# Taking the float64 weight conversion of an attention and MoE kernel in sixths of its columns

## The chip, the cores and the metric

The kernel runs on one core of one Trainium2 chip. The time is the device time of one execution in microseconds; the number to predict is the median of several runs of the changed kernel.

## The reference, cut to what matters

```python
# attention: q, k, v are (4, 12, 448, 64) float32
scores = scale * q @ k^T, causal mask, softmax over the last axis
attn_out = attn @ v
# MoE with a rational activation: x is (1792, 768)
x = attn_out.transpose(0, 2, 1, 3).reshape(1792, 768)
h = x @ w_in                        # w_in (768, 2048), float64
P = a0 + a1*h + a2*h^2 + a3*h^3
Q = 1 + |b0|*|h| + |b1|*h^2
g = P / (Q + 1e-6)
out = (g @ w_out).astype(float32)   # w_out (2048, 768), float64
```

The two weight matrices come as float64. The kernel reads them as pairs of 32-bit words and builds float32 values from the words by hand.

## The kernel before, in words

The kernel has an attention stage and an MoE stage. The attention stage loops over 24 head pairs (`NP`), one iteration per pair, and each iteration issues a list of small tasks in the order of the string `ORDER` (`attend`, L947; the first three iterations use `FIRST`, `SECOND` and `THIRD`). A task `name.arg@lag` works on the pair of the iteration less the lag. So one iteration holds, for different pairs: transposes of q and k (`qk`, psA), the scores (`s`, psS, L328), their maxima on VectorE (`m`, L339), the exponentials on ScalarE (`e`, L349), the reciprocal of the sums on VectorE (`r`, L359, with a small GpSimd op ahead of it, L356), the scaling of the exponentials on GpSimd (`n`, seven instructions, L366), their transposes on TensorE (`c`, psC, L385) with copies out of PSUM on VectorE (`v`, L397) and ScalarE (`a`, L395), the product with v (`d`, psD, L409) and its transfer to the MoE input (`dh` on ScalarE, `dl` on VectorE, L437 and L439).

Beside this, the attention stage converts the first weight blocks ("items") from float64 to float32. One item is a block of 128 x 768 values, loaded as `raw`, 128 x 768 x 2 words (`conv_load`, L143, three buffers). It takes two steps, `n` = 2 and `n` = 3 in the list `steps` (L444). Step 2 needs a GpSimd op on `raw` (L169, it leaves the sign in `u`) and then one VectorE instruction (L179) that joins the low word's top bits to `u`. Step 3 needs a GpSimd op (L173, it scales the high word in place by a power of two) and then one VectorE instruction (L185) that joins the shifted high word to `u`. Both VectorE instructions have two inputs in SBUF.

Which steps belong to which iteration is told by `quota` (L441): one whole step in iterations 3 to 15, 17, 19 and 21, and none in the others, 16 steps in all (eight items; items 8 and 9 are converted in the list `TAIL`). In an iteration the GpSimd op of its step is issued early (`cv.0`), which on GpSimd's queue is right behind the seven scalings of the iteration before; the VectorE instruction is issued last (`cv.2`), so on VectorE it stands between the last maximum and the next iteration's copies of psC. `cv.1` takes the first half of the iteration's steps, which is none where there is one. When an item is finished, the buffer is free and the load of the item three later is issued in the next iteration (`cv.3`). All DMAs go through SyncE's queue, in program order. The order on each engine is the order of the tasks, since the stage is scheduled by hand (`manual_schedule`, L893).

The MoE stage follows with matmuls that keep TensorE busy to the end, with the remaining weight blocks converted beside them.

Of the kernel before, what the change touches and what calls it, by code (L numbers as in the profile page):

```python
# [8 lines left out]
F32 = mybir.dt.float32  # L9
F32R = mybir.dt.float32r  # L10
U32 = mybir.dt.uint32
AF = mybir.ActivationFunctionType
ALU = mybir.AluOpType
# [3 lines left out]

ORDER = """
c.1@2 e.6@1 c.0@2 e.0@1 lv@-1 v.1@2 cv.0 dh@3 qk@-1 ld@-4 cv.3 a.1@2 sm@1 v.0@2 s.2 a.0@2 r@1 dl@3 qy@-1 n.2@1 s.3 qx@-1
n.3@1 m.3 m.4 s.0 n.5@1 s.1 e.3 m.5 d@2 n.0@1 e.4 n.4@1 m.0 e.5 m.1 n.6@1 m.2 e.1 m.6 n.1@1 e.2 cv.1 cv.2  # L20
"""


# [36 lines left out]
def kernel(  # L60
# [11 lines left out]
    nc = tc.nc  # L72
    B, H, S, D = q.shape
    DM, DFF = moe_w_in.shape
    P = 128
# [12 lines left out]
    NC = 10  # L88
    NR = 3
    NL = 3  # L90
# [6 lines left out]
    cv = ctx.enter_context(tc.tile_pool(name="cv", bufs=1))  # L97
# [43 lines left out]
    c_raw, c_u, c_32, stored = {}, {}, {}, set()  # L141

    def conv_load(m):  # L143
        if m >= len(items):
            return
        f, n = items[m]
        raw = c_raw[m] = cv.tile([P, DM, 2], U32, tag="raw", bufs=NR, name="raw64")
        if n == 0:
            nc.sync.dma_start(
                out=raw.rearrange("p (c f) t -> p c (f t)", c=KD),  # L150
                in_=moe_w_in[:, f * P:(f + 1) * P].bitcast(U32).rearrange("(c p) f -> p c f", p=P),
            )
        else:
            nc.sync.dma_start(
                out=raw.rearrange("p m t -> p (m t)"), in_=moe_w_out[f * P:(f + 1) * P, :].bitcast(U32)
            )

    def conv_step(m, s):
        raw = c_raw[m]
        yu = raw[:, :, 1]  # L160
        y = yu.bitcast(F32)
        if s == 1:
            if m in kept:
                u = xq.tile([P, K3 * NT], U32, tag=f"c{kept.index(m)}", name="u")[:, :DM]
            else:
                pool, tag, bufs = (lv, f"u{m}", 1) if NL <= m < NC - 3 else (cv, "u", 3)
                u = pool.tile([P, DM], U32, tag=tag, bufs=bufs, name="u")
            c_u[m] = u
            nc.gpsimd.tensor_scalar(  # L169
                out=u.bitcast(F32), in0=y, scalar1=0.0, scalar2=1.0, op0=ALU.mult, op1=ALU.mult  # L170
            )
        elif s == 5:
            nc.gpsimd.tensor_scalar(  # L173
                out=y, in0=y, scalar1=2.0 ** -112, scalar2=1.0, op0=ALU.mult, op1=ALU.mult
            )
        elif s == 4:
            nc.scalar.activation(out=y, in_=y, func=AF.Copy, scale=2.0 ** -112)
        elif s == 2:
            nc.vector.scalar_tensor_tensor(  # L179
                out=c_u[m], in0=raw[:, :, 0], scalar=29, in1=c_u[m],  # L180
                op0=ALU.logical_shift_right, op1=ALU.bitwise_or,
            )
        else:
            o = cv.tile([P, DM], F32, tag="ld", bufs=NL, name="w").bitcast(U32) if m < NL else c_u[m]
            nc.vector.scalar_tensor_tensor(  # L185
                out=o, in0=yu, scalar=3, in1=c_u[m], op0=ALU.logical_shift_left, op1=ALU.bitwise_or
            )
            c_32[m] = o.bitcast(F32)

    def conv_store(m):  # L190
        nc.sync.dma_start(out=w32[items[m]], in_=c_32[m])
# [58 lines left out]
    raw, QK, AT, pv, SUM, REC, psa, pss, psr, psc, nmx = {}, {}, {}, {}, {}, {}, {}, {}, {}, {}, {}  # L250
# [25 lines left out]
    def half(j):  # L276
        return slice(j * D, (j + 1) * D)
# [155 lines left out]
    def d_lo(p):  # L433
        ps = pv.pop(p)
        for r, hi, o in x_parts(p):
            if hi is not None:
                nc.vector.tensor_tensor(out=o, in0=ps[:, r], in1=hi.bitcast(F32), op=ALU.subtract)  # L437
            elif p % 2 == 0:
                nc.vector.tensor_copy(out=o, in_=ps[:, r])  # L439

    def quota(p):  # L441
        return int(3 <= p < 16 or p in (17, 19, 21))

    steps = [(m, n) for m in range(NC) for n in (2, 3)]  # L444
    done = []

    def conv(p, part):
        if part == 0:
            lo = sum(quota(x) for x in range(p))
            for m, n in steps[lo:lo + quota(p)]:  # L450
                conv_step(m, 1 if n == 2 else 5)
        elif part == 3:
            while done:
                conv_load(done.pop(0) + NR)
        else:
            lo = sum(quota(x) for x in range(p))
            mid, hi = lo + quota(p) // 2, lo + quota(p)
            for m, n in steps[lo:mid] if part == 1 else steps[mid:hi]:
                conv_step(m, n)
                if n == 3:  # L460
                    done.append(m)

    tasks = {
# [2 lines left out]
        "s": stage_b_pe, "m": stage_b_max, "e": stage_b_exp, "sm": stage_b_sum, "r": stage_b_rec, "n": stage_b_norm,  # L466
        "c": c_pe, "a": lambda p, h: c_ev(p, h, 0), "v": lambda p, h: c_ev(p, h, 1),
        "d": stage_d, "dh": d_hi, "dl": d_lo, "cv": conv,
    }

# [15 lines left out]
    tmp, g_t, acc, osb, part = {}, {}, {}, {}, {}  # L486
# [370 lines left out]
    def coeffs_done():  # L857
# [5 lines left out]
        "co": coeffs_done, "xr": close_r, "xl": close_l, "p1": p1, "p2": p2, "aa": act_a, "da": dve_a, "dz": dve_a3,  # L863
        "ab": act_b, "db": dve_b, "dy": dve_b3, "gh": g_hi, "gl": g_lo, "wh": w_hi, "wl": w_lo,
        "lw": load_w, "xa": lambda m: conv_step(m, 1), "xc": conv_step, "xs": conv_store, "xd": conv_load,
    })

# [25 lines left out]
    with tc.manual_schedule():  # L893
# [12 lines left out]
        ld = es_r.enter_context(pool(name="ld", bufs=2, side="right"))  # L906
# [7 lines left out]
        for x in range(2):  # L914
            m = mask[half(x), S - QB:]
            nc.gpsimd.affine_select(
                out=m, in_=m, compare_op=ALU.is_ge, fill=-1e9 / SCALE, base=0, pattern=[[-1, QB]], channel_multiplier=1,
# [51 lines left out]
        for t in range(2, NPL - 1):  # L969
            now = step.get(t, [])  # L970
# [57 lines left out]
        for j in range(HF):  # L1028
            n = j + 5
# [46 lines left out]
```

## Time and profile before

| | |
|---|---|
| median of 3 runs | 602.48 us (602.44 to 602.89) |
| the profiled execution | 602.94 us |
| its span | 601.1 us |
| TensorE busy | 594.0 us (99%) |
| VectorE busy | 535.9 us (89%) |
| ScalarE busy | 448.6 us (75%) |
| GpSimd busy | 169.2 us (28%) |
| TensorE's granted clock | 1.00 in both stages |

The span is the part of the execution that the profile covers. In the profile PE is TensorE, DVE is VectorE, ACT is ScalarE, POOL is GpSimd and SPq is the queue of SyncE, from which the DMAs are issued. A tile is named as the program names it, without its buffer number; L179 is line 179 of the kernel. Times of instructions are counted from the start of the span.

### The profile page before, as it was taken

Reading aid. Unit: us, or ns where it says so; the run is one execution under the profiler, and the core shown is the slowest. Engines: PE = TensorE matmul, PEld = TensorE weight load, DVE = VectorE, ACT = ScalarE, POOL = GpSimd, SP = SyncE. Lnnn points to the kernel's source line nnn. Section 1 sums busy time; section 2 is a strip of 40 time slices with the busy share of each in tenths; the row PEclk is TensorE's granted clock in tenths of the full one; section 3 lists DMA queues with packets and bytes.
Section 4 is the critical chain, followed back from the end, with each engine's and each line's share of the span. In section 5 each row is a group of like instructions: output and inputs, shape, how many; then the busy total and the mean of one; then the engine's idle time right before and its main releaser. Section 6 shows DMA issues by size and latency. Waiting matters only on the chain.

```text
span 601.1 us, 12762 instructions
## 1 busy us (share of the span) xinstructions
PE 594.0 (99%) x4660; PEld 494.2 (82%) x4660; DVE 535.9 (89%) x1015; ACT 448.6 (75%) x923; POOL 169.2 (28%) x266
## 2 busy tenths in 40 slices
PE   8999999999999999999999999999999999999997
PEld 6666666667888888888888888889999999998886
DVE  3999999988799999999999879998999999988950
ACT  4999999998877776668777776676477777677731
POOL 2899997766733401112333100000000000000000
PEclk9999999999999999999999999999999999999999
DMA  7979898776389988888985663443353344149872
GB/s 163 234 180 228 182 204 210 181 194 224 149 284 347 336 304 288 298 308 301 358 297 183 225 217 139 158 139 125 135 206 132 109 154 145 66 184 339 294 254 85
DMA packets 104863, 128.64 MB, mean 214 GB/s; under 512 B 70496, under 2 KB 82912, under 8 KB 104800
## 3 DMA queue, kind: packets, MB, share of 16 engines
q1 hardware_dynamic: 104800, 127.82, 67.2%
q8 instruction: 37, 0.61, 0.4%
q14 instruction: 26, 0.21, 0.1%
HBM read 98.31 MB, written 29.49 MB: 213 GB/s over the span
## 4 chain that ended last, share of the span: by engine, by line
PE 95%; DVE 2%; ACT 1%; POOL 1%; issue 0%; ACTq 0%
PE psO L614 25%; PE psH L242 22%; PE psQ L728 14%; PE psM L610 13%; PE psD L409 7%; PE psS L328 7%; PE psC L385 4%; PE psA L296 2%; PE psI L943 1%; ACT e L349 1%; POOL e L366 0%; DVE wq L707 0%; DVE xparts L637 0%; DVE p L528 0%; DVE at L397 0%
## 5 line engine op out<-in xcount | busy, mean ns | idle before, releaser
L614 PE MATMUL psO<-whl,gh 128*128 128x512 f32 x448 | 159.1, 391 | 0.0
L242 PE MATMUL psH<-xs,whl 128*128 128x512 f32 x576 | 136.7, 391 | 0.2 <-ACT e L349 0.2
L610 PE MATMUL psM<-whl,gh 128*128 128x256 f32 x448 | 126.2, 282 | 0.0
L242 PEld LDWEIGHTS psH<-xs,whl 128*128 128x128 f32 x576 | 105.9, 188 | 21.9 <-ACT e L349 0.3
L614 PEld LDWEIGHTS psO<-whl,gh 128*128 128x128 f32 x448 | 84.0, 188 | 17.8 <-ACT gh L540 0.4
L610 PEld LDWEIGHTS psM<-whl,gh 128*128 128x128 f32 x448 | 84.5, 189 | 1.7 <-DVE osb L598 0.3
L349 ACT ACTIVATE e<-psS,nm 128x448 f32<-128x448 f32 (+6 forms) x168 | 79.3, 568 | 4.3 <-DVE nm L339 3.2
L614 PE MATMUL psO<-whl,gl 128*128 128x512 f32 x224 | 81.1, 390 | 0.0
L728 PE MATMUL psQ<-xpart,wq 128*128 128x384 f32 x432 | 78.5, 336 | 0.1
L366 POOL TENSOR_SCALAR e<-e,r 128x192 f32<-128x192 f32 (+6 forms) x161 | 74.4, 487 | 13.9 <-DVE r L359 9.4
L728 PEld LDWEIGHTS psQ<-xpart,wq 128*128 128x128 f32 x432 | 74.8, 188 | 1.4 <-DVE hpair L754 0.4
L339 DVE CUSTOM_DVE_ANT_0 psS<-psS,mask 128x64 f32<-128x64 f32 (+6 forms) x168 | 65.4, 456 | 1.8 <-PE psS L328 1.3
L610 PE MATMUL psM<-whl,gl 128*128 128x256 f32 x224 | 63.2, 282 | 0.0
L169 POOL TENSOR_SCALAR u<-raw 128x768 f32<-128x768 f32 x32 | 36.9, 1153 | 57.6 <-DMA raw<-in_moe_w_out_dram 25.0
L517 ACT ACTIVATE w<-w 128x512 f32<-128x512 f32 x32 | 20.3, 633 | 39.8 <-DVE w L502 39.8
L614 PEld LDWEIGHTS psO<-whl,gl 128*128 128x128 f32 x224 | 42.0, 188 | 8.9
L328 PE MATMUL psS<-qkt 64*64 64x64 f32 (+6 forms) x672 | 47.5, 391 | 1.4 <-ACT e L349 1.2
L349 ACT ACTIVATION_READ_ACCUMULATOR e<-psS,nm 128x1 f32 x168 | 48.5, 299 | 0.0
L409 PE MATMUL psD<-at,vraw 128*64 128x448 f32 (+3 forms) x384 | 46.8, 386 | 0.0
L409 PEld LDWEIGHTS psD<-at,vraw 128*64 128x64 f32 x384 | 25.5, 136 | 24.9 <-issue 14.8
L610 PEld LDWEIGHTS psM<-whl,gl 128*128 128x128 f32 x224 | 42.3, 189 | 0.0
L328 PEld LDWEIGHTS psS<-qkt 64*64 64x64 f32 x672 | 21.3, 132 | 20.4 <-ACT at L395 10.7
(111 smaller groups left out, 1117.1 us busy)
## 6 DMA issues: line engine op xcount, KB each, us to landing
whl<-whl SPq DMA_DIRECT2D x64, 768.0 KB, 5.5
w<-w SPq DMA_DIRECT2D x51, 384.0 KB, 5.1
raw<-in_moe_w_in_dram SPq DMA_DIRECT2D x16, 768.0 KB, 5.4
raw<-in_moe_w_out_dram SPq DMA_DIRECT2D x16, 768.0 KB, 6.1
w<-u SPq DMA_DIRECT2D x26, 384.0 KB, 3.4
qraw<-in_q_dram SPq DMA_DIRECT2D x48, 112.0 KB, 3.5
kraw<-in_k_dram SPq DMA_DIRECT2D x48, 112.0 KB, 3.7
out_dram<-osb SPq DMA_DIRECT2D x13, 384.0 KB, 3.1
```

Source lines behind the costliest of these rows:

```text
L169: nc.gpsimd.tensor_scalar(out=u.bitcast(F32), in0=y, scalar1=0.0, scalar2=1.0, op0=ALU.mult, op1=ALU.mult)
L242: nc.tensor.matmul(ps, w[:, c * P:(c + 1) * P], xs[ck, part, c // K3][:, c % K3], start=(c == 0 and n == 0), stop=(c == KD - 1 and n == 2),)
L328: nc.tensor.matmul(pss[p, b][half((1 + b + j) % 2)], QK[p][half(j), 0, b * QB:(b + 1) * QB], QK[p][half(j), 1, :b_w[b]], start=True, stop= ...
L339: nc.vector.tensor_tensor_reduce(out=s, in0=s, in1=mask[:, S - w:], scale=-SCALE, scalar=3e38, op0=ALU.add, op1=ALU.min, accum_out=nmx[p][ ...
L349: nc.scalar.activation(out=E[p % 2][i][:, :w], in_=pss[p, i], func=AF.Exp, bias=nmx[p][:, i:i + 1], scale=-1.0, accum_out=SUM[p % 2][:, i: ...
L366: nc.gpsimd.tensor_scalar(out=e, in0=e, scalar1=REC[p][:, i:i + 1], scalar2=0.0, op0=ALU.mult, op1=ALU.add)
L385: nc.tensor.transpose(ps[x][:, slot // 2 * QB:(slot // 2 + 1) * QB], E[p % 2][n][r, lo:lo + P], ident[r, r])
L409: nc.tensor.matmul(ps[half(j), lo * QB:S], v[:, j, c], a[h][:, slot * QB:(slot + 7 - lo) * QB], start=(c == 0), stop=(c == 3), skip_group_ ...
L517: nc.scalar.activation(out=w, in_=w, func=AF.Abs)
L610: nc.tensor.matmul(acc["m", k], g, w[:, 512:], start=first and (k % 2 == 0 or each), stop=last, skip_group_check=True)
L614: nc.tensor.matmul(acc[k], g, w[:, :512], start=first, stop=last)
L728: nc.tensor.matmul(q_bank[j, bank], w[:, wp_, c * P:(c + 1) * P], xp_[:, c], start=(first and n == 0), stop=(n == 3 * K3 - 1), skip_group_ ...
```

## The change

The two VectorE instructions of a step can now be issued for a part of the columns, from `lo` to `hi`. The list `steps` holds each step six times, once for each sixth of its 768 columns, and `quota` counts sixths: five in iterations 3 to 12, six in 13, 14, 15, 17, 19 and 21, four in 16, three in 18 and 20 (96 sixths, the same 16 steps). In an iteration the sixths of one step are joined to one VectorE instruction; where an iteration's sixths belong to two steps, there are two instructions. The GpSimd op still covers all columns and is issued in the iteration in which the step begins. In iteration 18 the scaling of step 3 is done by VectorE (step number 6) ahead of its piece, and GpSimd has no such op. `cv.1`, which did nothing, is gone.

```diff
--- before.py
+++ after.py
@@ -17,7 +17,7 @@
 
 ORDER = """
 c.1@2 e.6@1 c.0@2 e.0@1 lv@-1 v.1@2 cv.0 dh@3 qk@-1 ld@-4 cv.3 a.1@2 sm@1 v.0@2 s.2 a.0@2 r@1 dl@3 qy@-1 n.2@1 s.3 qx@-1
-n.3@1 m.3 m.4 s.0 n.5@1 s.1 e.3 m.5 d@2 n.0@1 e.4 n.4@1 m.0 e.5 m.1 n.6@1 m.2 e.1 m.6 n.1@1 e.2 cv.1 cv.2
+n.3@1 m.3 m.4 s.0 n.5@1 s.1 e.3 m.5 d@2 n.0@1 e.4 n.4@1 m.0 e.5 m.1 n.6@1 m.2 e.1 m.6 n.1@1 e.2 cv.2
 """
 
 
@@ -155,9 +155,9 @@
                 out=raw.rearrange("p m t -> p (m t)"), in_=moe_w_out[f * P:(f + 1) * P, :].bitcast(U32)
             )
 
-    def conv_step(m, s):
+    def conv_step(m, s, lo=0, hi=DM):
         raw = c_raw[m]
-        yu = raw[:, :, 1]
+        yu = raw[:, lo:hi, 1]
         y = yu.bitcast(F32)
         if s == 1:
             if m in kept:
@@ -169,23 +169,25 @@
             nc.gpsimd.tensor_scalar(
                 out=u.bitcast(F32), in0=y, scalar1=0.0, scalar2=1.0, op0=ALU.mult, op1=ALU.mult
             )
-        elif s == 5:
-            nc.gpsimd.tensor_scalar(
+        elif s in (5, 6):
+            (nc.gpsimd if s == 5 else nc.vector).tensor_scalar(
                 out=y, in0=y, scalar1=2.0 ** -112, scalar2=1.0, op0=ALU.mult, op1=ALU.mult
             )
         elif s == 4:
             nc.scalar.activation(out=y, in_=y, func=AF.Copy, scale=2.0 ** -112)
         elif s == 2:
             nc.vector.scalar_tensor_tensor(
-                out=c_u[m], in0=raw[:, :, 0], scalar=29, in1=c_u[m],
+                out=c_u[m][:, lo:hi], in0=raw[:, lo:hi, 0], scalar=29, in1=c_u[m][:, lo:hi],
                 op0=ALU.logical_shift_right, op1=ALU.bitwise_or,
             )
         else:
-            o = cv.tile([P, DM], F32, tag="ld", bufs=NL, name="w").bitcast(U32) if m < NL else c_u[m]
+            if lo == 0:
+                o = cv.tile([P, DM], F32, tag="ld", bufs=NL, name="w") if m < NL else c_u[m].bitcast(F32)
+                c_32[m] = o
             nc.vector.scalar_tensor_tensor(
-                out=o, in0=yu, scalar=3, in1=c_u[m], op0=ALU.logical_shift_left, op1=ALU.bitwise_or
-            )
-            c_32[m] = o.bitcast(F32)
+                out=c_32[m][:, lo:hi].bitcast(U32), in0=yu, scalar=3, in1=c_u[m][:, lo:hi],
+                op0=ALU.logical_shift_left, op1=ALU.bitwise_or,
+            )
 
     def conv_store(m):
         nc.sync.dma_start(out=w32[items[m]], in_=c_32[m])
@@ -438,26 +440,37 @@
             elif p % 2 == 0:
                 nc.vector.tensor_copy(out=o, in_=ps[:, r])
 
+    NQ = 6
+
     def quota(p):
-        return int(3 <= p < 16 or p in (17, 19, 21))
-
-    steps = [(m, n) for m in range(NC) for n in (2, 3)]
+        if 3 <= p < 13:
+            return 5
+        if p in (13, 14, 15, 17, 19, 21):
+            return 6
+        return {16: 4, 18: 3, 20: 3}.get(p, 0)
+
+    steps = [(m, n, i) for m in range(NC) for n in (2, 3) for i in range(NQ)]
     done = []
 
     def conv(p, part):
+        lo = sum(quota(x) for x in range(p))
+        now = steps[lo:lo + quota(p)]
         if part == 0:
-            lo = sum(quota(x) for x in range(p))
-            for m, n in steps[lo:lo + quota(p)]:
-                conv_step(m, 1 if n == 2 else 5)
+            for m, n, i in now:
+                if i == 0 and p != 18:
+                    conv_step(m, 1 if n == 2 else 5)
         elif part == 3:
             while done:
                 conv_load(done.pop(0) + NR)
-        else:
-            lo = sum(quota(x) for x in range(p))
-            mid, hi = lo + quota(p) // 2, lo + quota(p)
-            for m, n in steps[lo:mid] if part == 1 else steps[mid:hi]:
-                conv_step(m, n)
-                if n == 3:
+        elif part == 2:
+            runs = {}
+            for m, n, i in now:
+                runs.setdefault((m, n), []).append(i)
+            for (m, n), r in runs.items():
+                if p == 18:
+                    conv_step(m, 6)
+                conv_step(m, n, r[0] * DM // NQ, (r[-1] + 1) * DM // NQ)
+                if n == 3 and r[-1] == NQ - 1:
                     done.append(m)
 
     tasks = {
```

## Rows read from the trace of the kernel before

**Rows 1.** The chain of waits, from the page: shares of the span by engine.

```profile
PE 95%; DVE 2%; ACT 1%; POOL 1%; issue 0%; ACTq 0%
```

**Rows 2.** Windows: us, busy us (instructions) by engine, granted clock, DMA share, GB/s.

```profile
69.64:75.17 5.53, 5.53 (x94) 3.49 (x96) 5.53 (x21) 5.53 (x22) 5.04 (x10) 1.00 0.91 173
107.88:113.27 5.39, 5.39 (x94) 3.62 (x96) 4.47 (x20) 5.39 (x20) 4.38 (x10) 1.00 0.70 155
137.80:594.00 456.20, 456.09 (x2470) 402.52 (x2471) 411.09 (x555) 319.37 (x468) 63.65 (x46) 1.00 0.63 219
```

**Rows 3.** VectorE by time, iteration 11: start, us, engine, line, op, out<-in [idle before].

```profile
71.32 1.09 DVE L179 SCALAR_TENSOR_TENSOR u<-raw,u 128x768 uint32<-128x768 uint32 x1
72.33 1.27 DVE L397 COPY at<-psC 128x512 f32<-128x512 f32 x2
73.53 0.20 DVE L359 RECIPROCAL r<-r 128x7 f32<-128x7 f32 x1
73.65 0.64 DVE L437 TENSOR_TENSOR xs<-psD,xs 128x64 fp32r<-128x64 f32 x2
```

**Rows 4.** GpSimd by time, the same iteration.

```profile
68.39 3.22 POOL L366 TENSOR_SCALAR e<-e,r 128x192 f32<-128x192 f32 x7 [0.41 <-DVE r L359]
71.57 1.64 POOL L173 TENSOR_SCALAR raw<-raw 128x768 f32<-128x768 f32 x1
```

**Rows 5.** VectorE by time, iteration 18.

```profile
109.41 0.14 DVE L339 DVE_READ_ACCUMULATOR2_ANT nm<- 128x1 f32 x1
110.47 1.29 DVE L397 COPY at<-psC 128x512 f32<-128x512 f32 x2 [0.92 <-PE psC L385]
```

**Rows 6.** GpSimd by time, iteration 18.

```profile
109.88 0.93 POOL L169 TENSOR_SCALAR u<-raw 128x768 f32<-128x768 f32 x1
```

**Rows 7.** VectorE by time, iteration 5: xs in one piece.

```profile
40.61 0.57 DVE L437 TENSOR_TENSOR xs<-psD,xs 128x448 fp32r<-128x448 f32 x1
```

**Rows 8.** VectorE's groups by shape, 300 to 601 us: busy us, mean ns | idle before.

```profile
L534 DVE SCALAR_TENSOR_TENSOR p<-w,p 128x512 f32<-128x512 f32 x13 | 8.9, 687 | 0.3
...
L689 DVE TENSOR_TENSOR s<-w 128x384 f32<-128x384 f32 x16 | 8.8, 553 | 0.2
...
L185 DVE SCALAR_TENSOR_TENSOR u<-raw,u 128x768 uint32<-128x768 uint32 x4 | 3.8, 948 | 0.0
```

**Rows 9.** VectorE by time, where GpSimd's op comes, MoE stage.

```profile
139.03 0.94 DVE L225 TENSOR_TENSOR whl<-w,whl 128x768 fp32r<-128x768 f32 x1
139.89 1.63 DVE L179 SCALAR_TENSOR_TENSOR u<-raw,u 128x768 uint32<-128x768 uint32 x1
...
249.51 1.64 DVE L185 SCALAR_TENSOR_TENSOR u<-raw,u 128x768 uint32<-128x768 uint32 x1
...
265.15 0.95 DVE L185 SCALAR_TENSOR_TENSOR u<-raw,u 128x768 uint32<-128x768 uint32 x1
266.02 1.39 DVE L534 SCALAR_TENSOR_TENSOR p<-w,p 128x512 f32<-128x512 f32 x1
```

**Rows 10.** GpSimd by time, the same places.

```profile
139.05 1.66 POOL L169 TENSOR_SCALAR u<-raw 128x768 f32<-128x768 f32 x1
...
249.45 0.88 POOL L169 TENSOR_SCALAR u<-raw 128x768 f32<-128x768 f32 x1 [6.97 <-DMA raw<-in_moe_w_out_dram]
...
265.67 1.19 POOL L169 TENSOR_SCALAR u<-raw 128x768 f32<-128x768 f32 x1 [8.14 <-DVE p L528]
```

**Rows 11.** VectorE's groups, whole span: the one-input cast.

```profile
L217 DVE CAST whl<-w 128x768 fp32r<-128x768 f32 x1 | 0.6, 556 | 0.0
```

**Rows 12.** DMA issues, from the page: KB each, median us to landing.

```profile
raw<-in_moe_w_out_dram SPq DMA_DIRECT2D x16, 768.0 KB, 6.1
```

**Rows 13.** SyncE's queue by time: the load issued in iteration 11.

```profile
76.48 0.43 SPq L149 DMA_DIRECT2D raw<-in_moe_w_in_dram  x1
```

**Rows 14.** GpSimd by time: the op of iteration 14.

```profile
82.59 1.62 POOL L173 TENSOR_SCALAR raw<-raw 128x768 f32<-128x768 f32 x1
```

**Rows 15.** DMA issues, 65.0 to 65.5 us: one raw load.

```profile
raw<-in_moe_w_out_dram SPq DMA_DIRECT2D x1, 768.0 KB, 6.7
```

## The prediction, on record before the change was run

> **What bounds the kernel now.** I read the chain of waits first: 95% of the span lies on TensorE and 2% on VectorE [rows 1], so time can be won or lost only where another engine holds TensorE up. The change lies in the attention stage, 24 head pairs of which one iteration lasts about 5.5 us, so I next cut that stage into stretches, each from one psD group of TensorE to the next. The stretch of 69.64 to 75.17 lasts 5.53 us and VectorE is busy in all of it; the stretch of 107.88 to 113.27, whose iteration (18) has no conversion step on VectorE, lasts 5.39 us [rows 2]. TensorE's own work is thus about 5.39 us, and iterations with a step are held by VectorE for up to 0.14 us more: over the twelve iterations 3 to 14 that is at most 1.7 us, all that this change could win.
>
> Then VectorE's instructions by time. In iteration 11 the step (L179) is issued at 71.32, the two copies of psC follow at 72.33, the reciprocal at 73.53 and the xs pieces at 73.65, each as soon as the one before allows [rows 3]. VectorE is the bound there, and whatever lengthens this row lengthens the iteration.
>
> Last, GpSimd beside it. Its seven scalings of e start at 68.39 and take 3.22 us; its conversion op is issued at 71.57, right behind them, and takes 1.64 us [rows 4], though the same op takes 0.93 us at 109.88, where VectorE has no step [rows 6]. The two engines stand in each other's way: VectorE's step waits for the last scaling (it takes 1.09 us against 0.95 us alone [rows 3, 8]), and GpSimd's op waits until VectorE's step is through.
>
> **The change part by part.** The pieces, in columns of 768, follow from the quotas:
>
> - iterations 3, 8, 9: one piece of 640; 16: one of 512; 20: one of 384; 17 and 21: a whole step
> - 4 and 10: 128 and 512; 5 and 11: 256 and 384; 6 and 12: 384 and 256; 7: 512 and 128
> - 13, 14, 15: 512 and 256; 19: 384 and 384
> - 18: the scaling of all 768 columns, taken from GpSimd, and a piece of 384
>
> Columns: 768 take 0.948 us and 384 take 0.553 us [rows 8], 1.03 ns a column, so 128 columns fewer save 0.13 us.
>
> Second instruction: xs in one piece of 448 takes 0.57 us [rows 7], in two pieces of 64 and 384 it takes 0.64 us [rows 3]: 0.07 us for one more instruction, if nothing comes between.
>
> What comes between is the point. From 139 to 267 us there are seven places where GpSimd's op is issued while VectorE runs an instruction with both inputs in SBUF and has another such instruction right behind. In all seven GpSimd runs in between, and the second VectorE instruction is longer by about its work; the first and the last are shown. At 139.03 VectorE runs L225, GpSimd's op comes at 139.05, and the next VectorE instruction takes 1.63 us for 0.95. At 265.15 it runs L185, GpSimd's op comes at 265.67, and L534 takes 1.39 us against 0.69 [rows 8 to 10]. The excess is 0.68 and 0.70 us; I take 0.68. How short a lead is enough: at 249.45 GpSimd's op is issued 0.06 us before L185, which then takes 1.64 us [rows 9, 10].
>
> In the attention stage the order is: last scaling, VectorE's step, and behind it GpSimd's op, which belongs to the step that begins in the next iteration. With one VectorE instruction, GpSimd gets its turn while VectorE copies from PSUM, and that hides it. With two, its turn falls between them. The op is there in time: the scalings end at 68.39 + 3.22 = 71.61, the op was issued at 71.57, and the first piece, held up until about 71.32 + 0.14 = 71.46, lasts 0.13 us for 128 columns and more for the others [rows 3, 4]. For 128 columns the lead is some 0.1 us, the closest case.
>
> Whether a GpSimd op stands behind the pieces: one is issued in every iteration in which a step begins, apart from 18, so none in 8, 16, 18 and 20; the pieces of 7, 15, 17 and 19 have none behind them. This leaves:
>
> - 4, 5, 6, 10, 11, 12: -0.13 + 0.07 + 0.68 = +0.62 us each, six times, 3.72 us
> - 13, 14: all columns in two pieces, 0.07 + 0.68 = +0.75 us each, 1.50 us
> - 3, 8, 9: -0.13 us, of which TensorE's own pace lets about 0.10 through: -0.30 us
> - 7: -0.13 + 0.07 = -0.06 us
> - 15, 19: 0.07 us each, at most partly seen; I take 0.07 for both
> - 16, 20: VectorE is idle in iteration 18 before the copies, from 109.41 + 0.14 to 110.47 (0.92 us) [rows 5], and 16 and 20 have the same gap; pieces of 512 and 384 (about 0.69 and 0.55 us, and 0.14 for the last scaling) fit: 0
> - 18: scaling and half a step go into the same gap, which counted from issue to issue is 110.47 - 109.41 = 1.06 us. The trace has no such scaling on VectorE. Nearest rows: a one-input cast of 768 columns in SBUF, 0.556 us [rows 11], and the two-input step, 0.948 us [rows 8]. With the half step (0.55 us) this is 1.1 to 1.5 us, and GpSimd's op of the next iteration, issued at 109.88 [rows 6], comes before the half step and adds up to 0.68: from 0 to 1.1 us late. I take 0.7: the half step can't begin before that op is through, at 109.88 + 0.93 = 110.81, and it ends near 111.3 less the 0.08 by which neighbours overlap.
>
> A page of the Trainium skill gives a price for this scaling. VectorE: DVE Perf Modes, What auto-detection actually checks, says that an op with a single source, source and destination both in SBUF and the outermost extent even runs at two elements a cycle, and that would hold here in spite of the stride of two. By it the scaling takes the 0.556 us of the cast, but (Mode 2x_2P, the same page) it uses both read ports, so that it too would wait for the last scaling; the sum for iteration 18 would be 0.95 instead of 0.7, the total a quarter of a microsecond more. No row shows a strided case.
>
> Loads: steps end later, so the raw loads are issued one or two iterations later. The tightest is item 5: issued in iteration 11, in the slot that holds another load at 76.48 now, median landing 6.1 us, and wanted by GpSimd in iteration 14, at 82.59 now [rows 12 to 14]. That is 6.11 us against 6.1: a tie, and at 6.7 us, which one such load took [rows 15], 0.6 us late. But iterations 12 and 13 grow by 1.4 us by the sum above and give it that margin, so 0. If they don't grow, 0 to 0.6 us. The other moved loads keep several us by the same count. The stores in iterations 20 to 22 come after the same last steps as before.
>
> Sum: 3.72 + 1.50 - 0.30 - 0.06 + 0.07 + 0.70 = 5.63 us. The profiled execution took 602.94 us with a span of 601.1, 0.46 above the median of 602.48. What attention loses is passed on whole, since from 137.8 to 594 us TensorE is busy in 456.09 of 456.20 us [rows 2]. So 608.6 in terms of the profiled execution, 608.1 as a median.
>
> **The rivals.**
> (a) *VectorE keeps its turn between two pieces.* Then the change does what its quotas suggest: -0.13 (3, 8, 9) and -0.06 us (4 to 7, 10 to 12), +0.07 (13, 14), and iteration 18 late by up to 0.4: about -0.30 - 0.42 + 0.14 + 0.2 = -0.4, so 602.1; with the late load 602.7, and with no cost in 18 and the pieces back to back for nothing 601.1. It decides if GpSimd asks for its turn later than I read it. For it: its issue and its asking need not be one moment, and only short pieces are new here. Against it: all seven places.
> (b) *Only the longer first pieces let GpSimd in.* With 128 columns VectorE goes on first: 4 and 10 give -0.06 instead of +0.62, so -1.36 us: 606.7. With 256 columns too soon as well, 5 and 11 go the same way: 605.4.
> (c) *The gap in 18 takes all of it:* -0.7 us, 607.4, a shade of the forecast.
>
> **How the numbers follow.** Forecast with its shade (c): 0.66; (b): 0.16; (a): 0.18, of which 0.05 for its fast end. A measurement of this kernel tells about 0.2% (1.2 us) from no change. Faster by more than that needs the fast end of (a): 0.05. Within it lies the rest of (a): 0.13. Slower: 0.82. The likeliest case alone spans 606.7 to 609.2. The range runs from 604.4, below (b), to 609.8, where 15 and 19 show and 18 costs its full bound.
>
> **What would show it.** Right: the second piece of 4 to 6 and 10 to 14 lasts 0.68 us longer than its columns need, GpSimd's conversion op is shorter than 1.6 us there, and those iterations last about 6.1 us, while 7 lasts 5.45 and 3, 8, 9 about 5.4. Wrong: second pieces of 0.3 to 0.7 us by their columns, GpSimd's op lengthened over both pieces, and no iteration beyond 5.5 us. Iteration 18 is judged by how late the copies of psC start behind TensorE's psC. If GpSimd waits for a raw load in iteration 14, I have misjudged the loads.

## The result, and the profile after

The changed kernel takes 608.7 us (608.51 to 608.96) against 602.53 us (602.44 to 602.89) of the kernel before beside it: a ratio of 1.0106, with a 95% interval of 1.0094 to 1.0119. The profiled execution's span went from 601.1 to 607.2 us.

On the page of the changed kernel, the shares of engines (busy us, share, instructions) and the chain of waits show where the 6 us went. TensorE's share of the chain fell from 95% to 86%, VectorE's rose from 2% to 10% [rows 1].

```profile
PE 599.1 (99%) x4660; PEld 497.2 (82%) x4660; DVE 543.9 (90%) x1030; ACT 449.3 (74%) x923; POOL 165.6 (27%) x265
...
PE 86%; DVE 10%; issue 2%; ACT 1%; POOL 1%; DVEq 0%; ACTq 0%
```

Windows of the changed kernel, columns as in [rows 2]: iterations 7, 11 and 18, then the MoE stage. They run from one start of VectorE's copies of psC to the next, where the windows of [rows 2] run from psD to psD; cut like these, iteration 11 grew from 5.50 to 6.13 us and 18 from 5.31 to 6.29. In 11 VectorE is busy throughout, as it was before; in 18 it now is in all but 0.2 us, where it was idle for 0.92 us [rows 5]. In the MoE stage TensorE is busy in 455.88 of 456.00 us, as before, so what attention lost was passed on.

```profile
46.49:51.91 5.42, 5.37 (x77) 3.17 (x78) 5.42 (x22) 4.85 (x17) 3.35 (x8) 1.00 0.79 226
68.92:75.05 6.13, 6.13 (x104) 4.07 (x100) 6.13 (x23) 5.87 (x22) 4.63 (x10) 1.00 0.69 155
110.13:116.42 6.29, 6.29 (x124) 4.39 (x120) 6.08 (x22) 6.29 (x25) 4.86 (x10) 1.00 1.03 253
144.00:600.00 456.00, 455.88 (x2470) 402.30 (x2469) 410.68 (x554) 319.23 (x468) 64.71 (x46) 1.00 0.62 218
```

VectorE of the changed kernel by time (columns as in [rows 3]): the pieces of iterations 4, 7, 11 and 18, with the copies of psC behind them.

```profile
32.56 0.39 DVE L179 SCALAR_TENSOR_TENSOR u<-raw,u 128x128 uint32<-128x128 uint32 x1
32.88 1.41 DVE L187 SCALAR_TENSOR_TENSOR w<-raw,u 128x512 uint32<-128x512 uint32 x1
...
50.92 0.87 DVE L187 SCALAR_TENSOR_TENSOR w<-raw,u 128x512 uint32<-128x512 uint32 x1
51.70 0.28 DVE L179 SCALAR_TENSOR_TENSOR u<-raw,u 128x128 uint32<-128x128 uint32 x1
51.91 1.28 DVE L399 COPY at<-psC 128x512 f32<-128x512 f32 x2
...
73.41 0.53 DVE L179 SCALAR_TENSOR_TENSOR u<-raw,u 128x256 uint32<-128x256 uint32 x1
73.87 1.26 DVE L187 SCALAR_TENSOR_TENSOR u<-raw,u 128x384 uint32<-128x384 uint32 x1
75.05 1.28 DVE L399 COPY at<-psC 128x512 f32<-128x512 f32 x2
...
114.61 0.70 DVE L173 TENSOR_SCALAR raw<-raw 128x768 f32<-128x768 f32 x1
115.34 1.15 DVE L187 SCALAR_TENSOR_TENSOR u<-raw,u 128x384 uint32<-128x384 uint32 x1
```

GpSimd of the changed kernel by time, the same iterations (none is issued in 7).

```profile
32.79 0.96 POOL L169 TENSOR_SCALAR u<-raw 128x768 f32<-128x768 f32 x1
...
73.64 1.07 POOL L169 TENSOR_SCALAR u<-raw 128x768 f32<-128x768 f32 x1
...
111.69 3.19 POOL L368 TENSOR_SCALAR e<-e,r 128x192 f32<-128x192 f32 x7 [0.94 <-DVE xs L439]
114.86 1.23 POOL L169 TENSOR_SCALAR u<-raw 128x768 f32<-128x768 f32 x1
```

Read the two together. In iteration 11 VectorE's first piece is issued at 73.41, GpSimd's op at 73.64, while that piece runs, and the second piece, issued at 73.87, takes 1.26 us, though 384 columns take 0.55 [rows 8]. GpSimd's op takes 1.07 us, where it took 1.64 when it had to wait for the end of one long instruction [rows 4]. In iteration 7 nothing of GpSimd's stands behind the pieces, and the second takes 0.28 us.

### The profile page after: what moved, and what is told of

It reads as the page before. It is cut to its first block, busy times and chain, and to the rows that moved or that the text cites. A ratio compares the mean times of both kernels' runs of the same rounds, so it can differ in the third digit from the quotient of the medians.

```text
span 607.2 us, 12775 instructions
## 1 busy us (share of the span) xinstructions
PE 599.1 (99%) x4660; PEld 497.2 (82%) x4660; DVE 543.9 (90%) x1030; ACT 449.3 (74%) x923; POOL 165.6 (27%) x265
## 4 chain that ended last, share of the span: by engine, by line
PE 86%; DVE 10%; issue 2%; ACT 1%; POOL 1%; DVEq 0%; ACTq 0%
PE psO L627 25%; PE psH L244 22%; PE psQ L741 14%; PE psM L623 13%; PE psS L330 4%; PE psD L411 4%; DVE psS L341 3%; PE psC L387 3%; DVE at L399 1%; DVE u L179 1%; PE psA L298 1%; PE psI L956 1%; ACT e L351 1%; DVE nm L341 1%; DVE u L187 1%
## 5 line engine op out<-in xcount | busy, mean ns | idle before, releaser
L351 ACT ACTIVATE e<-psS,nm 128x448 f32<-128x448 f32 (+6 forms) x168 | 77.9, 511 | 10.5 <-DVE nm L341 5.5
L330 PE MATMUL psS<-qkt 64*64 64x64 f32 (+6 forms) x672 | 51.0, 391 | 1.7 <-ACT e L351 1.2
L330 PEld LDWEIGHTS psS<-qkt 64*64 64x64 f32 x672 | 23.8, 132 | 22.8 <-DVE at L399 8.0
L179 DVE SCALAR_TENSOR_TENSOR u<-raw,u 128x768 uint32<-128x768 uint32 (+5 forms) x39 | 42.3, 1086 | 0.0
```

What stands on the lines that cost most here:

```text
L179: nc.vector.scalar_tensor_tensor(out=c_u[m][:, lo:hi], in0=raw[:, lo:hi, 0], scalar=29, in1=c_u[m][:, lo:hi], op0=ALU.logical_shift_right, ...
L330: nc.tensor.matmul(pss[p, b][half((1 + b + j) % 2)], QK[p][half(j), 0, b * QB:(b + 1) * QB], QK[p][half(j), 1, :b_w[b]], start=True, stop= ...
L351: nc.scalar.activation(out=E[p % 2][i][:, :w], in_=pss[p, i], func=AF.Exp, bias=nmx[p][:, i:i + 1], scale=-1.0, accum_out=SUM[p % 2][:, i: ...
```

## The experiments

The main measure is the length of an iteration: from the start of VectorE's copies of psC to the same point one iteration later, in VectorE's timeline. "No op in after" is the changed kernel without GpSimd's conversion ops.

| iteration | before | after | no op in after | piece behind copies (no scaling in 18) | one piece each | piece in the middle |
|---|---|---|---|---|---|---|
| 3 | 5.51 | 6.11 | 5.40 | 5.39 | 5.51 | 5.39 |
| 4 | 5.51 | 6.15 | 5.56 | 5.56 | 5.49 | 5.56 |
| 5 | 5.50 | 6.15 | 5.46 | 5.75 | 5.51 | 6.28 |
| 8 | 5.52 | 5.34 | 5.47 | 5.55 | 5.27 | 6.28 |
| 9 | 5.50 | 5.50 | 5.51 | 5.49 | 5.56 | 5.34 |
| 11 | 5.50 | 6.13 | 5.53 | 5.74 | 5.52 | 6.29 |
| 14 | 5.50 | 6.28 | 5.54 | 5.58 | 5.51 | 6.26 |
| 16 | 5.26 | 5.20 | 5.25 | 5.52 | 5.32 | 6.27 |
| 17 | 5.51 | 5.65 | 5.60 | 5.69 | 5.83 | 5.48 |
| 18 | 5.31 | 6.29 | 5.69 | 5.37 | 5.38 | 5.27 |
| 19 | 5.51 | 5.55 | 5.54 | 5.39 | 5.83 | 5.55 |
| 20 | 5.27 | 5.19 | 5.21 | 5.60 | 5.36 | 6.28 |

The theory throughout: a VectorE instruction with two SBUF inputs and GpSimd's op take turns, and an op that is issued while the first of two VectorE pieces runs goes ahead of the second.

**Without GpSimd's op.** In both kernels, for items 0 to 7:

```diff
-            nc.gpsimd.tensor_scalar(
+            if m >= 8:
+                nc.gpsimd.tensor_scalar(
...
+        elif s == 5 and m < 8:
+            pass
```

VectorE's step 2 then takes its second input from `raw`, since `u` is not written; it still has two inputs in SBUF.

The changed kernel:

> The changed kernel without GpSimd's conversion ops on the eight items of the attention stage (the sign and the scaling of these items are left out; VectorE's pieces keep their number, columns and places). If the loss is GpSimd's turn between two pieces, it goes: the pieces cost by their columns, iterations 4 to 6 and 10 to 12 fall from 6.1 to about 5.4 us, and the time is 602.0, between 601.3 and 602.8. If the loss lies in the pieces themselves, in the later loads or in the scaling that iteration 18 does on VectorE, most of it stays: 607 or more, for the last alone 603.

The kernel before:

> The kernel before with the same GpSimd ops left out, as the yardstick of the run above. With one piece an iteration the op is hidden beside the copies from PSUM, so by the theory nothing is won: 602.5, give or take 0.4. If the ops cost something in their own right, 601 or less, and the run above has to be read against that.

Measured: 602.91 against 602.3 us, ratio 1.0009 (0.9995 to 1.0024), and for the kernel before 602.37, ratio 1.0008 (0.9997 to 1.0018). The first is 0.1 us above the range that I expected, and iterations 4 to 6 and 10 to 12 fall to 5.46 to 5.56 us, not to 5.4. Without the op the pieces cost nothing that can be told, while taking it from the kernel before wins nothing: before, it was hidden. VectorE by time in the changed kernel without the op, iteration 11, has both pieces at the duration of their columns:

```profile
70.83 0.53 DVE L182 SCALAR_TENSOR_TENSOR u<-raw 128x256 uint32<-128x256 uint32 x1
71.28 0.55 DVE L190 SCALAR_TENSOR_TENSOR u<-raw,u 128x384 uint32<-128x384 uint32 x1
71.86 1.29 DVE L402 COPY at<-psC 128x512 f32<-128x512 f32 x2
```

**Two and three pieces in the order of before.** The kernel before with its own quotas, each step cut:

```diff
-            for m, n in steps[lo:mid] if part == 1 else steps[mid:hi]:
-                conv_step(m, n)
+            for m, n in now:
+                for i in range(NS):
+                    conv_step(m, n, i * DM // NS, (i + 1) * DM // NS)
```

With NS = 2:

> The schedule of the kernel before, one whole step in each of its 16 iterations, with nothing changed but that the VectorE instruction of a step is two of 384 columns. By the theory each of the twelve iterations 3 to 14 has a GpSimd op behind the pieces and grows by 0.07 + 0.68 = 0.75 us: 611.5, between 610 and 612.5. If only the second instruction's own cost counts, 16 times 0.07: 603.5 at most. The loads and iteration 18 are as before, so if those made the loss, 602.5.

With NS = 3:

> As the run with halves, with three instructions of 256 columns. There is one GpSimd op an iteration, so by the theory it takes one turn, at the first boundary after it is issued, and the third instruction adds only its own 0.07 us: twelve times 0.82, 612.4, about 0.9 above the halves. If every boundary costs by itself, whatever GpSimd does, twelve times 1.5: about 620.

Measured: 611.5 us with two pieces, ratio 1.0159 (1.0144 to 1.0174), and 612.21 with three, ratio 1.0178 (1.0155 to 1.02). Iterations 4 to 14 last 6.25 to 6.30 us with two and 6.33 to 6.36 with three, and 15, whose pieces have no op behind them, 5.55 and 5.62. So the price is one turn per iteration, about 0.7 us, however many boundaries there are, and 0.07 us for each more instruction. Two pieces, VectorE by time, iteration 9:

```profile
64.15 1.84 DVE L179 SCALAR_TENSOR_TENSOR u<-raw,u 128x384 uint32<-128x384 uint32 x2
65.91 1.27 DVE L399 COPY at<-psC 128x512 f32<-128x512 f32 x2
```

Three pieces, the same iteration:

```profile
66.86 1.93 DVE L179 SCALAR_TENSOR_TENSOR u<-raw,u 128x256 uint32<-128x256 uint32 x3
68.71 1.28 DVE L399 COPY at<-psC 128x512 f32<-128x512 f32 x2
```

**The scaling of iteration 18 back on GpSimd**, in the changed kernel:

```diff
-                if i == 0 and p != 18:
+                if i == 0:
...
-                if p == 18:
-                    conv_step(m, 6)
```

> The changed kernel with the scaling of iteration 18 given back to GpSimd. Its iteration 18 then has one piece of 384 columns, which fits into the gap before the copies of psC. In the trace of the changed kernel iteration 18 was 0.98 us longer than before, so the time should fall by 0.9, to about 1.009 times the kernel before. If that iteration's loss is only an echo of the late iterations before it, nothing changes: 1.0106.

Measured: 607.79 against 602.5 us, ratio 1.0092 (1.0078 to 1.0106). Iteration 18 lasts 5.37 us instead of 6.29. VectorE by time: the half step now takes 0.72 us (0.55 for its columns; the other 0.17 I read as the wait for the last scaling), and VectorE waits for TensorE again.

```profile
114.89 0.72 DVE L187 SCALAR_TENSOR_TENSOR u<-raw,u 128x384 uint32<-128x384 uint32 x1
115.79 1.29 DVE L399 COPY at<-psC 128x512 f32<-128x512 f32 x2 [0.19 <-PE psC L387]
```

**The second piece behind the copies of psC**, so that no two pieces are neighbours. In the list of tasks:

```diff
-... v.0@2 s.2 a.0@2 r@1 dl@3 ...
+... v.0@2 s.2 a.0@2 cv.1@1 r@1 dl@3 ...
```

In the changed kernel as it is:

> The changed kernel with the same pieces, the same GpSimd ops and the same loads, but the second piece of an iteration is issued behind the two copies of psC instead of directly behind the first piece. GpSimd's op then has its turn while VectorE copies from PSUM, as in the kernel before. If the loss is that turn, the eight iterations 4 to 6 and 10 to 14 fall from 6.1 or 6.3 to 5.5 us and only iteration 18 keeps its 0.98: 603.4, between 602.8 and 604.2. If the second instruction costs wherever it stands, 608 or more.

With the scaling of 18 on GpSimd as well:

> The two mends together: the second piece behind the copies, and GpSimd's scaling in iteration 18. If the loss of the change is these two places and nothing else, this is the kernel before within 0.1%: 602.3, and at best 601.8, since the runs without GpSimd's ops showed that shorter pieces win little. If something else is lost, 603.5 or more.

Measured: 605.18 against 602.5 us, ratio 1.0044 (1.003 to 1.0058), and 604.22, ratio 1.0034 (1.0022 to 1.0047). The lost turns are gone, but both are 1.8 to 1.9 us above what I expected, and the second lies where its "something else is lost" has it. VectorE by time, iteration 10 of the first, shows why the iterations don't come back to 5.5:

```profile
66.14 0.42 DVE L187 SCALAR_TENSOR_TENSOR w<-raw,u 128x128 uint32<-128x128 uint32 x1
67.16 1.29 DVE L399 COPY at<-psC 128x512 f32<-128x512 f32 x2 [0.60 <-PE psC L387]
68.36 0.68 DVE L179 SCALAR_TENSOR_TENSOR u<-raw,u 128x512 uint32<-128x512 uint32 x1
68.96 0.20 DVE L361 RECIPROCAL r<-r 128x7 f32<-128x7 f32 x1
```

The piece takes the 0.68 us of its 512 columns, but now stands ahead of the reciprocal and the maxima, and VectorE idles 0.60 us for psC: what it wins behind it gives back in front. Two things are in this, and the runs below settle the first: 9 to 13 can't fall below ScalarE's 5.52 us. Why some last 5.6 to 5.75 I read as the reciprocal and the maxima coming late; no run isolates that. These iterations are only half of the loss: in the second version 4 to 14 add up to 1.0 us, and 15 to 23 to 0.9, above all 16 and 20 (5.52 and 5.60 us instead of 5.26 and 5.27), in which the second pieces of 15 and 19 now stand.

**One piece per iteration**, half steps in 8 to 13 and whole ones in 3 to 7 and 14 to 21, no scaling on VectorE:

```diff
-        if 3 <= p < 13:
-            return 5
-        if p in (13, 14, 15, 17, 19, 21):
-            return 6
-        return {16: 4, 18: 3, 20: 3}.get(p, 0)
+        return 3 if 8 <= p < 14 else 6 if 3 <= p < 22 else 0
```

> The same 16 steps over the same 19 iterations 3 to 21, but never two pieces in one: whole steps in 3 to 7 and 14 to 21, halves in 8 to 13; all scalings on GpSimd. By the theory no turn falls between pieces: 602.3, give or take 0.5, where the six halves can win up to 0.1 us each if VectorE is the bound there, and the whole steps now in 16, 18 and 20 lose about as much. If spreading the steps, or the later loads that go with it, cost by themselves: 604 or more.

Measured: 603.73 against 602.5 us, ratio 1.0025 (1.0014 to 1.0036), 1.4 us above what I expected. With one piece no VectorE instruction loses its turn, but half steps win nothing in 9 to 13 (5.52 to 5.56 us; only 8 is shorter, 5.27). The whole steps fit the gaps of 16, 18 and 20, which last 5.32 to 5.38 us, under 0.1 more than before; but 17, 19 and 21 last 5.81 to 5.83 us instead of 5.51, and that makes 0.38 us per pair of iterations. VectorE, GpSimd and TensorE by time, at the end of iteration 16, show the turn the other way round:

```profile
98.32 0.97 DVE L179 SCALAR_TENSOR_TENSOR u<-raw,u 128x768 uint32<-128x768 uint32 x1
98.46 1.07 POOL L368 TENSOR_SCALAR e<-e,r 128x128 f32<-128x128 f32 x1
99.59 0.65 PE L387 MATMUL psC<-ident,e 64*128 64x64 f32 x14 [0.21 <-POOL e L368]
```

VectorE's step is issued 0.14 us before GpSimd's last scaling and takes the time of its columns; the scaling takes 1.07 us, where the same one takes 0.38 in the kernel before (at 98.77), and TensorE's transposes wait for it, in 18 and 20 as in 16. The changed kernel has a smaller case: behind the piece of iteration 16 the last scaling, at 103.65, takes 0.80 us, and 17 lasts 5.65.

VectorE by time, iteration 9, waits for TensorE:

```profile
59.88 0.67 DVE L187 SCALAR_TENSOR_TENSOR w<-raw,u 128x384 uint32<-128x384 uint32 x1
60.94 1.29 DVE L399 COPY at<-psC 128x512 f32<-128x512 f32 x2 [0.39 <-PE psC L387]
```

**What then holds 9 to 13 at 5.52?** I suspected a loop through VectorE's row (copies, reciprocal, xs, maxima), and took xs out of it:

```diff
-            if hi is not None:
+            if hi is not None and 6 <= p < 12:
+                continue
+            elif hi is not None:
```

> The kernel with one piece an iteration, with the low part of x left out for pairs 6 to 11 (set to zero at the start instead), so that VectorE's two xs instructions are missing in iterations 9 to 14. With half steps VectorE waited there for psC and an iteration still took 5.52 us. I now read a loop: psC 0.78 us to VectorE's first copy, 2.80 us of copies, reciprocal, xs and two maxima, 0.06 to psD, 1.89 us of psD to the next psC, 5.53 in all; a step behind the last maximum is not in it. By this the 0.55 us of xs go out of the loop, and iterations 9 to 13 fall to what is next, TensorE's own 5.39 or ScalarE's 5.43. If ScalarE's queue holds these iterations, they stay at 5.5.

Measured: 604.88 us, beside 602.72 of the kernel before (no interval), and 9 to 13 still last 5.52 us: the loop falls. ScalarE of this kernel by time shows another holder:

```profile
71.41 0.93 ACT L431 CAST xs<-psD 128x64 fp32r<-128x64 f32 x2
71.88 1.44 ACT L397 COPY at<-psC 128x512 f32<-128x512 f32 x2
72.83 1.36 ACT L313 COPY qkt<-psA 128x384 f32<-128x384 f32 x2
73.78 0.78 ACT L351 ACTIVATE e<-psS,nm 128x256 f32<-128x256 f32 x1
...
76.94 0.93 ACT L431 CAST xs<-psD 128x64 fp32r<-128x64 f32 x2
```

No row between has idle time before it, and from the casts of one iteration to those of the next it is 76.94 - 71.41 = 5.53 us, of which the casts are 0.47 (71.88 - 71.41). So I took these casts out for the same pairs, from the version with one piece and from the kernel before:

```diff
-            if hi is not None:
+            if hi is not None and 6 <= p < 12:
+                continue
+            elif hi is not None:
                 nc.scalar.copy(out=hi, in_=pv[p][:, r])
```

> One piece per iteration, as in the version of that name, with ScalarE's casts of psD into the high part of x left out for pairs 6 to 11 (iterations 9 to 14); the high part is zero there and VectorE still subtracts it. Theory: ScalarE itself holds iterations 9 to 13 at 5.52 us: its instructions are issued back to back through such an iteration, 5.52 us from one copy of psC to the next, of which the two casts are 0.47. Without them it needs 5.05 and VectorE 5.17, so TensorE's own 5.39 us is left: iterations 10 to 13 at 5.37 to 5.42. Rival: something other than ScalarE or VectorE holds them, and they stay at 5.52.

> The kernel before with the same casts left out. Theory: VectorE's row, with a whole step in each iteration, is as long as ScalarE's, so with ScalarE relieved VectorE still holds iterations 10 to 13 at 5.48 to 5.52 us, and the kernel takes the time of before within 0.5 us. Rival: ScalarE alone was the bound, VectorE's lack of idle time being only what it is stretched to: 5.39 to 5.42 us.

Measured: with one piece, iterations 10 to 13 last 5.39 to 5.40 us, in the kernel before 5.49 (602.67 and 602.69 us, beside 602.11 of the kernel before; no interval). The lengths are both as the theory has it; the time of the second is 0.58 us above the kernel before, where I expected 0.5 at most, but these are single executions. Without the casts and with half steps, the chain of waits of an iteration is TensorE alone, 1.14 + 0.50 + 1.88 + 1.88 = 5.40 us:

```profile
70.43 1.14 PE psC L387 x32
71.56 0.50 PE psA L298 x15
72.06 1.88 PE psS L330 x23
73.94 1.88 PE psD L411 x16
```

In the kernel before without the casts, a window (columns as in [rows 2]) has VectorE busy throughout and ScalarE no longer:

```profile
65.80:71.30 5.50, 5.50 (x100) 3.86 (x98) 5.50 (x21) 5.15 (x20) 5.00 (x10) 1.00 0.92 253
```

So iterations 10 to 13 of the kernel before are held twice, by VectorE at 5.49 us and by ScalarE at 5.52, with TensorE at 5.39 behind them: there a shorter step alone wins nothing. It isn't shown for the iterations ahead of 9, in which the casts are one instruction and not two, and 3 and 8 did get shorter with a shorter step.

The run without xs shows one thing more. Its iterations 14 and 19, of one whole step each, lasted 6.39 and 6.74 us. VectorE by time:

```profile
87.23 1.64 DVE L179 SCALAR_TENSOR_TENSOR u<-raw,u 128x768 uint32<-128x768 uint32 x1
...
115.83 1.79 DVE L187 SCALAR_TENSOR_TENSOR u<-raw,u 128x768 uint32<-128x768 uint32 x1
```

GpSimd by time:

```profile
87.14 0.93 POOL L173 TENSOR_SCALAR raw<-raw 128x768 f32<-128x768 f32 x1
...
112.68 3.20 POOL L368 TENSOR_SCALAR e<-e,r 128x192 f32<-128x192 f32 x7 [0.55 <-DVE r L361]
115.85 0.95 POOL L169 TENSOR_SCALAR u<-raw 128x768 f32<-128x768 f32 x1
```

A single piece loses its turn too where it comes 0.09 us after GpSimd's op, or 0.02 before it, while the last scaling still runs (to 112.68 + 3.20 = 115.88). In the kernel before VectorE is 0.25 us ahead, 71.32 against 71.57, and wins [rows 3, 4].

**The second piece in the middle of the maxima**, on the kernel with the piece behind the copies and the scaling of 18 on GpSimd:

```diff
-... a.0@2 cv.1@1 r@1 ...
-n.3@1 m.3 m.4 s.0 ...
+... a.0@2 r@1 ...
+n.3@1 m.3 m.4 cv.1@1 s.0 ...
```

> The kernel with both mends, with the second piece moved once more: behind the second maximum of the next iteration, which is outside the loop named above, but beside GpSimd's seven scalings. Two things are expected. The loop is not lengthened by the piece, so iterations 4 to 6 and 10 to 14 lose the 0.1 to 0.25 us that the piece cost behind the copies. And by the turns the piece meets a scaling under way: it lasts longer than its columns need (0.28 to 0.68 us) by up to one scaling, 0.46. VectorE's row is then 5.5 plus some 0.2 us, so the whole stays near the kernel with both mends, 603.5 to 605; without turns, 602.5.

Measured: 609.58 against 602.72 us, ratio 1.0119 (1.0103 to 1.0136): the worst place, 4.6 us beyond the range that I expected. VectorE by time, iteration 5:

```profile
35.58 0.96 DVE L187 SCALAR_TENSOR_TENSOR w<-raw,u 128x512 uint32<-128x512 uint32 x1
...
38.26 1.08 DVE L187 SCALAR_TENSOR_TENSOR w<-raw,u 128x256 uint32<-128x256 uint32 x1
39.27 1.28 DVE L399 COPY at<-psC 128x512 f32<-128x512 f32 x2
```

GpSimd by time:

```profile
34.56 3.63 POOL L368 TENSOR_SCALAR e<-e,r 128x192 f32<-128x192 f32 x7 [0.70 <-DVE r L361]
38.16 0.91 POOL L173 TENSOR_SCALAR raw<-raw 128x768 f32<-128x768 f32 x1
```

The middle piece meets a scaling and takes 0.96 us instead of 0.68, as expected. What I hadn't foreseen is that VectorE's row gets late against GpSimd's: the conversion op is issued at 38.16, 0.10 us before the last piece, which takes 1.08 us instead of the 0.41 of 256 columns. Such iterations last about 6.28 us, nine of them. It is the case of 249.45 [rows 9, 10] again.

## Why the prediction was right, by its own steps

- **The turn, the heart of the sum.** The second pieces of 4 to 6 and 10 to 14 are 0.71 to 0.74 us longer than their columns, forecast 0.68. Iterations 4 to 6 and 10 to 12 lost 0.61 to 0.67 us each, 3.82 in all (forecast 3.72), and 13 and 14 0.76 and 0.78 (forecast 1.50 for both). Rival (a) falls: without the op the loss is gone.
- **The closest case,** 128 columns: GpSimd's op at 32.79 comes 0.23 us after the first piece is issued and 0.09 before the second, and goes in between. Rival (b) falls, in iterations 4 and 10 as in 5 and 11.
- **Relief in 3, 8 and 9,** -0.30: 8 won 0.18 us, 9 nothing, and 3 about 0.14, hidden by the start-up. Iteration 3 began 0.83 us earlier than before (its copies start at 21.95 against 22.78) and lasted 6.11 us against 5.51: GpSimd's op sat until 22.61 behind 1.02 us of idle time, as I read it for the first raw load (issued at 15.73; with the scaling of 18 on GpSimd the same wait lasts until 22.82, and the profile names that load), and VectorE's reciprocal then waited for GpSimd. From the reciprocal to the next copies it is 28.06 - 23.89 = 4.17 us, before 28.29 - 23.98 = 4.31. Where the op didn't wait, with the piece behind the copies, iteration 3 lasts 5.39 us. So the size comes out, the reason for 9 only does not. The step that failed there is "iterations with a step are held by VectorE for up to 0.14 us more": ScalarE holds 9 to 13 as well, at 5.52 us, and its 5.53 of 5.53 stood in the same row [rows 2]. In these iterations relief of VectorE alone could win next to nothing, so the case of a gain (the fast end of (a)) was weaker than its 0.05.
- **Iteration 18,** +0.70: from the issue of the scaling to the copies of psC it took 116.42 - 114.61 = 1.81 us, where the gap was 1.06 [rows 5], so 0.75. The iteration grew by 0.98 us, as the row of maxima ahead of the gap was 0.23 longer (4.48 us from the copies to the gap, 4.25 before). It is so with the scaling on GpSimd as well (4.47), where the gap still hides it. The scaling itself was 0.70 us; less the 0.14 that a step in this place waits for the last scaling [rows 3, 8] this is 0.56, the cast's 0.556 [rows 11]. GpSimd's op behind it took 1.23 us for 0.93, and the half step 1.15 for 0.55. Without GpSimd's ops iteration 18 lasts 5.69 us, so the op's turn is 0.60 of the 0.98, and the scaling with the longer row 0.38; why the row is longer no run isolates. By the Trainium skill, VectorE: DVE Perf Modes, What auto-detection actually checks, a single source and a destination in SBUF with even outermost extents are enough for two elements a cycle, and the trace agrees in spite of the stride, 0.56 us. The 0.95 us that I worked out from it for the gap was 0.2 too long, and fits the iteration's 0.98 by chance. Rival (c) falls.
- **The small ones.** 7: -0.08 (forecast -0.06). 15 and 19: 0.06 for both (0.07). 16 and 20: -0.14 for both (0): their pieces fit the gaps. Not forecast: 17 and 22, +0.23 for both, of which 17 has 0.14; ahead of it the piece of 16 holds up GpSimd's last scaling, a cost of such a piece that the prediction put at nothing.
- **The loads** cost nothing that shows: the op of iteration 14 was issued behind the scalings, as in the others.

Together 3.82 + 1.54 - 0.41 (3, 8 and 9 with 0.09 of start-up) + 0.98 - 0.08 + 0.06 - 0.14 + 0.23 = 6.00 us, against 5.63 forecast; the first copies of psC behind iteration 23 start 5.99 us later (143.19 against 137.20), and the span grew by 6.1. The median came out at 608.7 us, forecast 608.1.

## What to carry to other kernels

Before you cut an instruction of VectorE in two, look at what GpSimd has queued at that moment: one long piece can shut out an op that is harmless behind it, and a boundary lets it in, at the price of most of the op's duration (here 0.71 to 0.74 of 0.93 us). The turn goes the other way too: a piece that gets ahead of a GpSimd instruction that TensorE waits for holds up TensorE. Cut work so that each place holds one piece, or put between the pieces something that GpSimd doesn't collide with, and check what then comes late. And where VectorE has no idle time, read the other engines' rows of the same window before you credit relief: a second one that is as full takes back whatever you save.

## What was not expected of the hardware

- The turn is worth the same in two or three pieces: 6.28 and 6.34 us an iteration. GpSimd gets one turn and VectorE's remaining pieces then run on; I read this as GpSimd having no further op ready.
- GpSimd's op gets faster by it, 0.96 to 1.35 us in the eight iterations with two pieces against 1.6 with one, which helps nobody: it isn't late in either kernel.
- An order that has held for a whole kernel can rest on 0.25 us: with the op 0.10 us ahead (38.16 against 38.26), or VectorE only 0.02 ahead (115.83 against 115.85), a single VectorE instruction was held up by 0.67 and 0.84 us.
